# A 480-byte unused tile beside the pre-split weights of the last stage, and that stage's four raw-block pools in the opposite order of SBUF

## The chip, the cores and the metric

The kernel runs on one core of a Trainium2 chip. The metric is the device time of one execution in microseconds (us); the median of three runs is given. The core has five instruction queues that run side by side and wait for each other by semaphores: TensorE (PE, matrix products), VectorE (DVE), ScalarE (ACT), GpSimd (POOL) and SyncE (SP, which here only issues transfers). SP and POOL issue DMA transfers strictly in the order of their queues: an issue that waits holds up every issue behind it. The working memory SBUF has 128 partitions; a place in it is given below as a byte address along the partition. Matrix products accumulate in PSUM.

## The reference

The output is the sum of the input, a spectral mixing of the normalised input, and a gated feed-forward layer of it, all in float32 with 2048 tokens, 640 features and 1728 hidden units:

```
xn = layernorm(x)
a, b = xn @ hid_re.T, xn @ hid_im.T
A = seq_re @ a - seq_im @ b
gate, up = xn @ W_gate, xn @ W_up
B = ((gate * (gate > 0)) * up) @ W_down
out = x + A + B
```

## The kernel before

Every float32 product is made from three matmuls of a shorter float format. An operand is split into a high part (a rounding copy, on ACT, line 125) and a low part (the rest, a subtraction on DVE, line 126); then `mm3` (lines 131 to 133) issues high by high, high by low, and low by high. Each of these matmuls has 128 by 128 stationary weights and 512 moving columns. Most products are further cut into seven block products in place of eight (names such as B11, T1, B21, T2, B22, T3, T4).

There are three stages. In the first, the sequence matrices are streamed and multiplied with the normalised tokens. In the second, `gate_up(n)` runs for 26 steps (13 blocks of hidden units for each half `q` of the tokens, first q = 1 and then q = 0), followed by `gate_up_rest(0, 25)` for the 64 left-over hidden units. In the third, `project(q)` multiplies what the first two stages left in DRAM (`pq`, `hd`, `hr`) with the hidden-DFT matrices and W_down, for q = 1 and then q = 0.

**The third stage.** `project` makes a list of units: the seven products in the order B11, T1, B21, T2, B22, T3, T4, each over 7 units (three of the hidden DFT: feature blocks 0-1, 2-3, 4; three of W_down; one `end`). A unit has a `load` (DMAs on SP), a `prepare` (differences and splits on DVE and ACT) and a `run` (matmuls). `drive(4, 2)` writes out the order for SP and POOL: loads four units ahead of the run, prepares two units ahead. The order on PE, DVE and ACT inside this stage is planned when the program is built; that of the second stage is the program order on these three.

A unit's data: a raw block `rw` of 128 x 1024 floats (4096 bytes a partition) in one of four pools `raws0` to `raws3`, six buffers each; its split form `cb` (pool `ring2`); and weights. For B11, T1, B21 and B22 the weights come as raw `wr` (pool `wraw`) and are split by ACT and DVE into `wt` (pool `wts`). For T2, T3 and T4 both parts come ready from DRAM (`wparts`, `wend`, which the second stage wrote through its tiles `pw`), by one DMA into `wd` (pool `wdir`, six buffers of 4096 bytes), and no engine touches them before PE. `y` holds the output blocks and `re` the raw blocks of the unit `end`.

Unit 0 of B11 for q = 1 is special: it is loaded and split early, in the second stage, by `lead_load` and `lead_split`, into the tile `gw` of that stage. So the first load of the third stage is that of unit 1: at line 1102 the raw block of unit 1, then (needed only later, by T1) that of unit 0, and at line 1155 the weights `wr` of unit 1.

**Places.** SBUF is filled from both ends; a pool takes the next bytes on its side. A place of the third stage lies where tiles of the second did, and its first transfer waits for the last use of whatever lay there. Two names occur twice: `wr` is also the left-over weights of the second stage (pool `wr`, read by PE in `gate_up_rest`), and `gw` exists at an even and an odd place. In the program before, the places are:

| second stage | bytes | third stage | bytes |
|---|---|---|---|
| gw, even steps | 2048 to 19456 | wr (raw weights) | 2048 to 14336 |
| st (left stage) | 19456 to 27648 | cb | 14336 to 47104 |
| r1 | 27648 to 60416 | wt | 47104 to 71680 |
| pw, two tiles | 60416 to 84992 | raws0 | 71680 to 96256 |
| p1, u2, u3 | 84992 to 91136 | raws1 | 96256 to 120832 |
| oa | 91136 to 95232 | raws2 | 120832 to 145408 |
| wr (left-over weights) | 95232 to 100352 | raws3 | 145408 to 169984 |
| ob | 100352 to 108544 | wd | 176096 to 200672 |
| z | 108544 to 128000 | y | 200672 to 221152 |
| st (stage3) | 128000 to 136192 | re | 221152 to 229344 |
| sets_b (T2, T1, T3, T4; 8192 each) | 136192 to 168960 | | |
| gw, odd steps | 170496 to 187904 | | |
| xs_early (B and X sets) | 187904 to 228864 | | |
| edge (480 bytes, unused) | 228864 to 229344 | | |

A pool of the third stage hands out its lowest buffer first and then goes from the highest down: for `raws0` 71680, 92160, 88064, 83968, 79872, 75776. Which pool a product's raw blocks take is `place` in `get`: for q = 1 B11, B12, B21, B22 take pools 0, 1, 2, 3; for q = 0 they take 3, 0, 1, 2.

Lines of the profile that the steps below speak of: 122, 125 and 126 (copies and splits), 131 to 133 (`mm3`), 856 (the last use of `oa`, in `finals`), 946, 947 and 950 (`gate_up_rest`: activation, product, store of `hr`), 1013 and 1017 (stores of `pw` to `wparts` and `wend`), 1037 and 1038 (`lead_load`), 1102 and 1108 (raw blocks), 1139, 1151 and 1155 (weights), 1210 (the two-matmul form of the last, short unit), 1233, 1236 and 1240 (`y`: load, addition, store).

Of the kernel before, what the change touches and what calls it, by code (L numbers as in the profile page):

```python
# [7 lines left out]
F32 = mybir.dt.float32  # L8
# [4 lines left out]
P = 128  # L13
# [11 lines left out]
LEDGE, EDGE = 448, 480  # L25
# [10 lines left out]
B11, B12, B21, B22, T1, T2, T3, T4, X4 = range(9)  # L36
# [22 lines left out]
def fnet_reglu_kernel(  # L59
# [490 lines left out]
    def first_stream(c, name, g):  # L550
# [7 lines left out]
        def load():  # L558
            if n == 0 and c == 0:
                st = start["raw"] = [raw(), raw()]  # L560
                get = lambda c, j: nc.sync.dma_start(st[c][:, j * CH : (j + 1) * CH], dft[c, 0, 0][:, j * CH : (j + 1) * CH])
                ln_load(0, slice(0, 1))
                get(0, 0)
                get(1, 0)
                ln_load(0, slice(1, 2))
                get(0, 1)
                get(1, 1)
                return
            if norm is not None:
                tc.keep_in_program_order(ln_load(norm, slice(0, SG)))  # L570
            if n > 0 or c > 1:
                t["s"] = raw()
                nc.sync.dma_start(t["s"], dft[c, 0, n])
                start[c, n] = t
# [191 lines left out]
    for step in range(2, SET_STEPS):  # L766
        load, (make, more), halve = token_sets(1, step)
        c, i = 1 + (step - 2) // 2, step % 2
# [41 lines left out]
    pool = open_pools.__getitem__  # L810
# [273 lines left out]
    ph0.close()  # L1084


    for n, b, side in (("wraw", 4, "left"), ("ring2", 4, "left"), ("wts", 4, "left"), *((f"raws{i}", 6, "left") for i in range(4)), ("ends", 4, "right"), ("y", 1, "right"), ("wdir", 6, "right")):
        open_pools[n] = ctx.enter_context(tc.tile_pool(name=n, bufs=b, side=side, reuse_waits="tile"))

    units = [("hid", u) for u in HID_UNITS] + [("f", u) for u in F_UNITS] + [("end", (NF // 2,))]  # L1090
    a, b2 = slice(0, REST), slice(REST, 2 * REST)
    raws, held = {}, []

    def get(q, kind, u):
        what, ks = units[u]
        place = (("B11", "B12", "B21", "B22").index(kind) + (3 if q == 0 else 0)) % 4
        o = raws[q, kind, u] = (pool("ends").tile([P, 1, CH], F32, name="re") if what == "end" else
                                pool(f"raws{place}").tile([P, 2, CH], F32, name="rw")[:, : len(ks)])
        col, row = int(kind in ("B12", "B22")), int(kind in ("B21", "B22"))
        cs = slice(col * CH, (col + 1) * CH)  # L1100
        if what == "hid":
            nc.sync.dma_start(o, pqd[2 * q + col][row][:, ks[0] : ks[-1] + 1])  # L1102
        elif what == "end" and row:
            if col:
                nc.gpsimd.memset(o[b2], 0.0)
            nc.sync.dma_start(o[a, 0], hrest[q][:, cs])
        else:
            nc.sync.dma_start(o, hd[q][2 * ks[0] + row : 2 * ks[-1] + row + 1 : 2][:, :, cs].rearrange("f p t -> p f t"))
# [211 lines left out]
```

## Time and profile before

| | |
|---|---|
| median of 3 runs | 1031.7 us (1031.12 to 1032.37) |
| the profiled execution, its own time | 1031.89 us |
| its span in the trace | 1030.1 us |
| PE busy | 1023.6 us, 99% of the span |
| weight loads (PEld) busy | 844.0 us, 82% |
| DVE, ACT, POOL busy | 818.1, 433.9, 124.8 us |
| granted TensorE clock | 1.0 |

The span runs from the first to the last recorded work; what lies around it in the profiled execution is 1031.89 - 1030.1 = 1.79 us. A row of the timeline has the start and the length in us, then engine, line, operation and tiles (written <- read). Matmuls overlap in the pipeline, so a row of 0.39 us does not mean that the next one starts 0.39 us later: the distance between two starts is what a matmul costs in a full stream. SPq rows are transfer issues on SP, not the transfers themselves.

### The profile page before, as it was taken

What the parts mean: (1) busy time and instruction counts of PE and PEld (TensorE: products, weight loads), DVE (VectorE), ACT (ScalarE), POOL (GpSimd) and SP (SyncE); (2) the same over time, 40 slices, a digit from 0 to 9 for tenths busy, and PEclk for the clock granted to TensorE, in tenths of its full rate; (3) what the DMA queues carried; (4) which work ended last, traced back from release to release, by engine and by line L of the source; (5) the groups of instructions that cost most, each with busy time, mean ns of one, the idle gap of its engine ahead of it and who ended that gap; (6) DMA issues with size and microseconds to landing.
All of it is one profiled execution on the core that took longest, in us unless ns stands there. A gap on an engine that the chain in (4) does not pass through costs nothing.

```text
span 1030.1 us, 12551 instructions
## 1 busy us (share of the span) xinstructions
PE 1023.6 (99%) x4520; PEld 844.0 (82%) x4520; DVE 818.1 (79%) x1117; ACT 433.9 (42%) x552; POOL 124.8 (12%) x196
## 2 busy tenths in 40 slices
PE   9999999999999999999999999999999999999998
PEld 7888888888888888888888888888788888888886
DVE  7967987998989585888778988886597895767973
ACT  5554453343433333433336434443454434444432
POOL 3531001012110002411100000011000000000000
PEclk9999999999999999999999999999999999999999
DMA  7897734968969784763464766774699467995724
GB/s 299 293 340 263 265 122 164 337 221 265 359 217 346 297 328 158 251 210 139 153 234 154 255 241 240 253 282 161 237 406 306 134 246 233 305 319 175 241 89 136
DMA packets 90525, 249.12 MB, mean 242 GB/s; under 512 B 11232, under 2 KB 30752, under 8 KB 87776
## 3 DMA queue, kind: packets, MB, share of 16 engines
q1 hardware_dynamic: 72288, 174.66, 49.6%
q0 software_dynamic: 18176, 73.67, 19.4%
q8 instruction: 35, 0.57, 0.2%
q14 instruction: 26, 0.21, 0.1%
HBM read 185.63 MB, written 61.62 MB: 240 GB/s over the span
## 4 chain that ended last, share of the span: by engine, by line
PE 99%; DMA 0%; DVE 0%; ACT 0%; SPq 0%; issue 0%
PE ps L131 31%; PE ps L133 31%; PE ps L132 31%; PE ps L498 3%; PE ps L527 1%; PE ps L1210 1%; PE ps L113 1%; DMA wr<-in_hid 0%; ACT wt L125 0%; DVE y L1236 0%; SPq L1102 0%; DVE warm L109 0%; DVE eps_t L103 0%
## 5 line engine op out<-in xcount | busy, mean ns | idle before, releaser
L125 ACT ACTIVATE cb<-rw 128x1024 fp32r<-128x1024 f32 x83 | 81.8, 987 | 136.2 <-PE ps L133 90.8
L126 DVE TENSOR_TENSOR cb<-rw,cb 128x1024 fp32r<-128x1024 f32 x83 | 93.9, 1132 | 50.9 <-ACT cb L125 50.1
L125 ACT ACTIVATE cb<-raw 128x1024 fp32r<-128x1024 f32 x71 | 75.3, 1060 | 114.8 <-PE ps L133 108.4
L126 DVE TENSOR_TENSOR cb<-raw,cb 128x1024 fp32r<-128x1024 f32 x71 | 86.8, 1223 | 40.0 <-ACT cb L125 39.7
L131 PE MATMUL ps<-cb,wt 128*128 128x512 f32 x270 | 105.2, 389 | 1.1 <-ACT wt L125 1.1
L132 PE MATMUL ps<-cb,wt 128*128 128x512 f32 x270 | 105.0, 389 | 0.0
L133 PE MATMUL ps<-cb,wt 128*128 128x512 f32 x270 | 104.9, 389 | 0.0
L131 PE MATMUL ps<-xs_early,gw 128*128 128x512 f32 x260 | 101.2, 389 | 0.0
L133 PE MATMUL ps<-xs_early,gw 128*128 128x512 f32 x260 | 101.2, 389 | 0.0
L132 PE MATMUL ps<-xs_early,gw 128*128 128x512 f32 x260 | 101.1, 389 | 0.0
L122 ACT ACTIVATE gw<-z 128x1024 fp32r<-128x1024 f32 (+1 forms) x52 | 57.7, 1110 | 79.5 <-DVE z L833 78.5
L131 PE MATMUL ps<-cb,xs_late 128*128 128x512 f32 x232 | 90.2, 389 | 0.0
L132 PE MATMUL ps<-cb,xs_late 128*128 128x512 f32 x232 | 90.2, 389 | 0.0
L133 PE MATMUL ps<-cb,xs_late 128*128 128x512 f32 x232 | 90.2, 389 | 0.0
L131 PE MATMUL ps<-cb,xs_early 128*128 128x512 f32 x226 | 87.9, 389 | 0.0
L132 PE MATMUL ps<-cb,xs_early 128*128 128x512 f32 x226 | 87.9, 389 | 0.0
L133 PE MATMUL ps<-cb,xs_early 128*128 128x512 f32 x226 | 87.9, 389 | 0.0
L122 ACT ACTIVATE u<-ps 128x512 f32<-128x512 f32 x52 | 31.1, 598 | 88.8 <-PE ps L133 88.8
L843 DVE TENSOR_TENSOR gw<-z,gw 128x1024 fp32r<-128x1024 f32 (+1 forms) x52 | 64.8, 1284 | 1.3 <-ACT gw L122 1.2
L131 PEld LDWEIGHTS ps<-cb,wt 128*128 128x128 f32 x270 | 50.7, 188 | 12.0 <-ACT wt L125 1.5
L133 PEld LDWEIGHTS ps<-cb,wt 128*128 128x128 f32 x270 | 50.7, 188 | 10.6
L132 PEld LDWEIGHTS ps<-cb,wt 128*128 128x128 f32 x270 | 50.7, 188 | 10.4
(191 smaller groups left out, 2216.3 us busy)
## 6 DMA issues: line engine op xcount, KB each, us to landing
raw<-in_dft SPq DMA_DIRECT2D x94, 512.0 KB, 6.1
z<-in_wgu SPq DMA_DIRECT2D x26, 640.0 KB, 3.9
wd<-wparts SPq DMA_DIRECT2D x30, 512.0 KB, 6.4
wparts<-pw POOLq DMA_DIRECT2D x12, 1152.0 KB, 4.4
hd<-ob POOLq DMA_DIRECT2D x26, 512.0 KB, 3.5
rw<-hd SPq DMA_DIRECT2D x24, 512.0 KB, 7.2
tk<-in_dft SPq DMA_DIRECT2D x16, 512.0 KB, 6.8
set<-r POOLq DMA_DIRECT2D x16, 512.0 KB, 4.0
```

Of the source, the lines that this page charges most:

```text
L113: nc.tensor.matmul(ps[:, :P], warm, warm, start=True, stop=True)
L122: return nc.scalar.activation(o, i, AF.Copy)
L125: nc.scalar.activation(hi, src, AF.Copy)
L126: return nc.vector.tensor_tensor(lo, src, hi.bitcast(F32), op=OP.subtract)
L131: nc.tensor.matmul(ps, wh, mh, start=first, stop=False, skip_group_check=more)
L132: nc.tensor.matmul(ps, wh, ml, start=False, stop=False, skip_group_check=more)
L133: nc.tensor.matmul(ps, wl, mh, start=False, stop=last, skip_group_check=more)
L498: start["pe"] = pin([nc.tensor.matmul(E[0, key], xn_part(n * SG + j, d)[v == 1], b[:, int(v == 2), j], start=False, stop=n % NH == NH - 1 ...
L527: pin([nc.tensor.matmul(E[c, key], xn_part(j, d)[v == 1], b[c][0][:, int(v == 2), j], start=j == 0 and v == 0, stop=False)])
L843: tt(self.w[:, 1, cs], self.z[:, cs], self.w[:, 0, cs].bitcast(F32), op=OP.subtract)
L1210: nc.tensor.matmul(B[out], w[:, 0, v, oo : oo + P], b[:, 0, 0], start=False, stop=last and v == 1, skip_group_check=more)
```

## The change

```diff
-    for n, b, side in (("wraw", 4, "left"), ("ring2", 4, "left"), ("wts", 4, "left"), *((f"raws{i}", 6, "left") for i in range(4)), ("ends", 4, "right"), ("y", 1, "right"), ("wdir", 6, "right")):
+    for n, b, side in (("wraw", 4, "left"), ("ring2", 4, "left"), ("wts", 4, "left"), *((f"raws{i}", 6, "left") for i in range(4)), ("ends", 4, "right"), ("y", 1, "right"), ("edge3", 1, "right"), ("wdir", 6, "right")):
...
+    pool("edge3").tile([P, EDGE // 4], F32, name="edge")
...
-        place = (("B11", "B12", "B21", "B22").index(kind) + (3 if q == 0 else 0)) % 4
+        place = (("B22", "B21", "B12", "B11").index(kind) + (q == 0)) % 4
```

`EDGE` is 480. The tile `edge` of the new pool `edge3` is never written or read; it takes 480 bytes on the right side between `y` and `wdir`, so that the six places of `wd` lie 480 bytes lower, at 175616 to 200192. `y` and `re` stay.

The raw blocks of B11, B12, B21 and B22 take pools 3, 2, 1, 0 for q = 1 and 0, 3, 2, 1 for q = 0: each old pool number p has become 3 - p. The pools themselves, their sizes and the order of loads, splits and matmuls in the program's text are the same.

## The prediction

> **What bounds the kernel now.** I read the busy shares first, then the chain of waits, then the waits of PE alone.
>
> ```profile
> span 1030.1 us, 12551 instructions
> PE 1023.6 (99%) x4520; PEld 844.0 (82%) x4520; DVE 818.1 (79%) x1117; ACT 433.9 (42%) x552; POOL 124.8 (12%) x196
> PE 99%; DMA 0%; DVE 0%; ACT 0%; SPq 0%; issue 0%
> PE ps L131 <- ACT wt L125: 1.1, 1, 1.1
> ```
>
> PE runs for 1023.6 of 1030.1 us, the chain that ended last is PE for 99%, and PE has one wait worth a name: 1.1 us for weights of the last stage. So only two things can move the time: what one matmul costs in the stream, and that wait. The grouping by line and shape shows that the first is not the same everywhere.
>
> ```profile
> L131 PE MATMUL ps<-cb,wt 128*128 128x512 f32 x270 | 105.2, 389 | 1.1 <-ACT wt L125 1.1
> L131 PE MATMUL ps<-xs_early,gw 128*128 128x512 f32 x260 | 101.2, 389 | 0.0
> L131 PE MATMUL ps<-cb,xs_early 128*128 128x512 f32 x226 | 87.9, 389 | 0.0
> L131 PE MATMUL ps<-cb,wd 128*128 128x512 f32 x140 | 55.0, 395 | 0.0
> ```
>
> All large groups take 389 ns a matmul, only those with weights in `wd` take 395. The timeline of PE shows what that is in the stream: here T2 of q = 1 begins, ends and gives way to B22, and here T3 and T4 do.
>
> ```profile
> 805.29 0.39 PE L131 MATMUL ps<-cb,wd 128*128 128x512 f32 x1
> ...
> 821.86 0.39 PE L133 MATMUL ps<-cb,wd 128*128 128x512 f32 x1
> 822.08 0.39 PE L131 MATMUL ps<-cb,wt 128*128 128x512 f32 x1
> ...
> 845.89 0.39 PE L131 MATMUL ps<-cb,wd 128*128 128x512 f32 x1
> ...
> 878.78 0.39 PE L133 MATMUL ps<-cb,wd 128*128 128x512 f32 x1
> 879.01 0.39 PE L131 MATMUL ps<-cb,wt 128*128 128x512 f32 x1
> ```
>
> T2 has 12 weight pairs, each for 2 outputs and 3 matmuls: 72 in 822.08 - 805.29 = 16.79 us, 0.2332 each. T3 and T4 have 72 and 70 (the short unit has 2 for 3): 142 in 33.12 us, 0.2332 again. B22 between them, weights in `wt`, has 11 x 9 + 6 = 105 in 845.89 - 822.08 = 23.81 us: 0.2268. So a matmul with `wd` costs 6.4 ns more.
>
> **The change, part by part.**
>
> *The unused tile.* It adds no instruction and no wait, and it moves `wd` from 176096 to 175616. A weight block is 512 bytes a partition and starts a multiple of 512 inside its tile, in `wd` as in `wt`. Of the table of places, `wt` (47104 = 92 x 512), both `gw` (2048, 170496) and `xs_early` (187904) lie on multiples of 512; 176096 is 480 past one, and 175616 is 343 x 512. The shift thus makes `wd` what all groups at 389 ns are. It isn't the height in SBUF: `gw` of the odd steps and `xs_early` lie on both sides of it, at 389. Bounds for a matmul with the shifted `wd`: 0.2332 (nothing changes) to 0.2268 (the row of `wt`). I take 0.2268, since in every other respect (type, size, stride, moving tile) `wd` is nearest to `wt`, in the same stage. T2: 16.79 - 72 x 0.2268 = 0.46 us; T3 and T4: 33.12 - 142 x 0.2268 = 0.91 us; twice, for both q: **2.75 us**. PE is the bound throughout, so all of it lies on the path; behind it DVE must keep up:
>
> ```profile
> 805.20:822.10 16.90, 16.90 (x75) 13.56 (x74) 14.72 (x18) 9.03 (x11) 1.66 (x3) 1.00 0.63 191
> 822.10:845.90 23.80, 23.80 (x107) 19.70 (x106) 22.34 (x26) 8.98 (x11) 0.00 (x0) 1.00 0.69 248
> 845.90:879.00 33.10, 33.10 (x143) 26.55 (x142) 22.09 (x25) 15.64 (x18) 2.70 (x5) 1.00 0.75 230
> ```
>
> Columns are the stretch, its length, then PE, PEld, DVE, ACT and POOL. DVE has 14.72 of 16.90 us in T2 and 22.09 of 33.10 in T3 and T4, so 0.46 and 0.91 us less still cover it. B22 with 22.34 of 23.80 is the tightest, but its time isn't shortened.
>
> The Trainium skill speaks against this part: "SBUF — State Buffer", section "Specifications (TRN2)", has lines of 16 bytes and a penalty for crossing into a new one. Both addresses are multiples of 16, so by it a block touches as many lines as before, and the gain of this part would be nothing; "TensorE: Matmul & The Clock Gate", section "Part 2: What happens when you issue a matmul", adds that loading the next weights takes no read bandwidth from the running matmul. The trace disagrees in the 6.4 ns, which neither page explains.
>
> *The pools in opposite order, where the second stage ends.* The raw blocks of B11 for q = 1 move from `raws0` to `raws3`. This is where PE's wait of 1.1 us comes from. SP's queue, its waits there, and PE:
>
> ```profile
> 718.81 12.63 SPq L1102 DMA_DIRECT2D rw<-pq  x2
> 731.49 0.43 SPq L1155 DMA_DIRECT2D wr<-in_hid  x1
> 731.96 0.46 SPq L1102 DMA_DIRECT2D rw<-pq  x1
> ...
> SPq L1102 <- DMA wend<-pw: 23.0, 1, 23.0
> SPq L1102 <- DVE ob L856: 8.4, 1, 8.4
> SPq L1102 <- PE ps L133: 3.5, 1, 3.5
> ...
> 723.88 0.39 PE L133 MATMUL ps<-sets_b,gw 128*128 128x512 f32 x1
> ...
> 730.68 0.39 PE L133 MATMUL ps<-xs_early,wr 128*128 128x512 f32 x1
> ...
> 735.01 0.39 PE L133 MATMUL ps<-gw 128*128 128x512 f32 x1
> 736.47 0.50 PE L131 MATMUL ps<-cb,wt 128*128 128x512 f32 x1 [1.07 <-ACT wt L125]
> 736.80 0.39 PE L132 MATMUL ps<-cb,wt 128*128 128x512 f32 x1
> ...
> 731.10 0.33 SPq L1102
> 731.49 4.06 DMA wr<-in_hid
> 735.57 0.85 ACT wt L125
> ```
>
> The first issue (unit 1, place 71680, inside both `pw`) went out at 718.81. The second (unit 0, place 92160 to 96256, across `oa` and the left-over `wr`) stood at the head of the queue until DVE line 856 had read `oa` and the last matmul on the left-over `wr` was done: 731.10, 0.42 us after that matmul's start. The weights of unit 1, whose own place had long been free, were queued behind it, went out at 731.49, took 4.06 us, then 0.85 us on ACT, and PE began late: 736.47 - 735.01 = 1.46 us, and 0.33 to the next, in place of 0.2268 each. That is **1.33 us** lost.
>
> After the change the two raw blocks lie at 145408 (in T1's part of `sets_b`) and 165888 (T4's). The last matmul on any part of `sets_b` starts at 723.88; with the same 0.42 us the queue is free at 724.3 at the latest. The weights are third, and issues follow each other by 0.47 (731.49, 731.96): out at 725.3, and landed at 729.4 by the 4.06 us. ACT gets to them behind its work of the second stage, if their order stays:
>
> ```profile
> 731.11 0.59 ACT L946 ACTIVATE st<-ps 64x512 f32<-64x512 f32 x1 [1.12 <-PE ps L133]
> 731.60 1.05 ACT L125 ACTIVATE cb<-rw 128x1024 fp32r<-128x1024 f32 x1
> ...
> 732.68 1.22 DVE L126 TENSOR_TENSOR cb<-rw,cb 128x1024 fp32r<-128x1024 f32 x1 [0.26 <-ACT cb L125]
> 736.45 0.96 DVE L126 TENSOR_TENSOR wt<-wr,wt 128x768 fp32r<-128x768 f32 x1 [2.54 <-ACT wt L125]
> ```
>
> ACT: high part of the weights from 732.65 to 733.5. DVE: low part from 733.9 to 734.9. PE wants the first at 735.01 + 0.23 = 735.24 and the second two matmuls later, so the wait is gone with 0.8 us to spare. Late next would be the splits of unit 2, but unit 1 gives PE 18 x 0.2268 = 4.1 us. I take the whole 1.33; the other bound is nothing, if ACT's order or another wait keeps PE at 736.47.
>
> *The pools elsewhere.* Inside the stage each old pool p is 3 - p for both q, so the same products follow each other in the same pool, and nothing changes but names. Against the second stage, B12 comes to `raws2`, where only 133120 (its fourth buffer) is late: `stage3`, from which `hr` is stored.
>
> ```profile
> 732.73 0.53 POOL L950 DMA_DIRECT2D hr<-st  x1 [4.24 <-DVE st L947]
> DMA to landing us min/median/max: 5.6/5.6/5.6
> 748.56 0.43 SPq L1108 DMA_DIRECT2D rw<-hd  x1
> ```
>
> The store lands at about 738.3, and the fourth unit of T1, which would now use that place, is loaded at 748.56, so 10 us cover it; uncovered it would cost SP's queue that difference. B21 and B22 come later still. The first `wd` places leave `xs_early` and lie under the odd `gw` alone, long free when they are loaded.
>
> *Sum.* 2.75 + 1.33 = 4.08 us off the profiled execution's 1031.89 (span 1030.1 and 1.79 around it): span 1026.0, execution 1027.8. That execution is 0.2 above the median, so the median becomes 1031.7 - 4.1 = **1027.6 us**.
>
> **The rivals.**
>
> *A. The shift does nothing; only the wait goes.* The 6.4 ns would come from something else that only `wd` has: no other weights are written by DMA alone. For it: the records of weight loads are no longer for `wd` (187 against 188 ns below). Against it: data that landed long ago can't tell who wrote it, and the pitch is 0.2332 in T2 and in T3 with T4, while the DMA share goes from 0.63 to 0.75 and ACT's share falls; contention would vary. Time: 1031.7 - 1.33 = 1030.4. The Trainium skill's line rule, above, gives this same time.
>
> ```profile
> L131 PEld LDWEIGHTS ps<-cb,wd 128*128 128x128 f32 x140 | 26.2, 187 | 6.6 <-DVE y L1236 0.3
> L133 PEld LDWEIGHTS ps<-cb,wt 128*128 128x128 f32 x270 | 50.7, 188 | 10.6
> ```
>
> *B. The wait stays, only the shift works.* The planner could put ACT's splits of unit 1 in another order, or another place could hold the queue as long. Time: 1031.7 - 2.75 = 1028.9.
>
> *C. The queue is held longer: slower.* One mechanism: the first raw block of `raws3` waits not for `sets_b` but for all of the second stage's tiles on that side, the store of `hr` among them (landing 738.3). With R the time of release, the weights go out at R + 0.95; PE's loss is 1.33 + (R + 0.95 - 731.49). It is nil up to R = 729.2, as before at 730.5, eats the gain of the shift at 733.3, and is measurably slower from 735.4. At R = 738.3 the loss grows by 7.8 and the time is 1031.7 - 2.75 + 7.8 = 1036.7. Against it: the present waits are for the very tiles that overlap (`pw`, `oa`, left-over `wr`), and `raws3` touches no part of `stage3` (136192 at most).
>
> *D. Neither part works*: 1031.7.
>
> **How the numbers follow.** Forecast (both) 0.80, A 0.06, B 0.07, C 0.04, D 0.03. A measurement of this kernel can tell about 0.2%, 2.1 us, from no change. Faster by more: forecast and B, 0.87; within: A and D, 0.09; slower: C, 0.04. Range: the runs before spread 0.6 below and 0.7 above their median. Low: 1027.6 - 0.6, and 0.2 since the execution that gives the terms is that much above the median: 1026.8. High: B's 1028.9 + 0.6 = 1029.5. That leaves A, C and D out, 0.13, and the tails.
>
> **What would show it.** Right: groups with `wd` at 389 ns; T2 in 16.3 us; no wait of PE at `wt` near 735; the `wr` issue at about 725. Wrong: `wd` still at 395 (A); PE's wait beside `wt` still 1 us or more, or the second line-1102 issue near 731 (B) or 738 (C); a new wait of PE later in the last stage, where there is none now, would say that the planner's order changed.

## The result and the profile after

| | before | after |
|---|---|---|
| median of 6 runs each | 1031.55 us (1031.00 to 1032.37) | 1027.51 us (1027.01 to 1030.23) |
| ratio, 95% interval | | 0.9964 [0.9951, 0.9976] |
| profiled execution, its own time | 1031.89 us | 1028.00 us |
| its span | 1030.1 us | 1026.1 us |

The forecast was 1027.6 us, span 1026.0. The change saves 0.36% of the time; the interval leaves no change out. After it, the page, the waits of PE and the groups by line and shape read:

```profile
span 1026.1 us, 12548 instructions
PE 1020.0 (99%) x4520; PEld 843.5 (82%) x4520; DVE 817.6 (80%) x1117; ACT 434.8 (42%) x552; POOL 125.1 (12%) x196
...
PE ps L113 <- DVE warm L109: 1.0, 1, 1.0
PE ps L131 <- ACT ob L122: 0.6, 1, 0.6
...
L131 PE MATMUL ps<-cb,wt 128*128 128x512 f32 x270 | 105.0, 389 | 0.0
L131 PE MATMUL ps<-cb,wd 128*128 128x512 f32 x140 | 54.3, 390 | 0.0
```

The groups with `wd` are at the duration of all others, and PE's wait for `wt` has gone. PE is busy for 3.6 us less in as many matmuls. T2 of q = 1 begins and gives way to B22 in the timeline at

```profile
804.02 0.39 PE L131 MATMUL ps<-cb,wd 128*128 128x512 f32 x1
...
820.34 0.39 PE L131 MATMUL ps<-cb,wt 128*128 128x512 f32 x1
```

which is 16.32 us for 72 matmuls, 0.2267 each, where 16.33 was forecast. The start of the last stage, on SP, ACT and PE:

```profile
724.03 0.39 PE L133 MATMUL ps<-sets_b,gw 128*128 128x512 f32 x1
...
724.45 0.81 SPq L1103 DMA_DIRECT2D rw<-pq  x2
725.36 0.38 SPq L1156 DMA_DIRECT2D wr<-in_hid  x1
...
730.39 0.85 ACT L125 ACTIVATE wt<-wr 128x768 fp32r<-128x768 f32 x1 [0.26 <-DMA wr<-in_hid]
731.25 0.60 ACT L946 ACTIVATE st<-ps 64x512 f32<-64x512 f32 x1
...
735.11 0.39 PE L133 MATMUL ps<-gw 128*128 128x512 f32 x1
735.34 0.39 PE L131 MATMUL ps<-cb,wt 128*128 128x512 f32 x1
```

(Lines below the new tile are one higher than before: 1103 is 1102, 1156 is 1155.) The weights of unit 1 go out at 725.36, the forecast was 725.3, and PE goes from the lead's last matmul to unit 1 in 0.23 us.

Two things in these two traces have nothing to do with the change. PE reaches the second stage at 156.96 us before and at 156.22 after, with the same code up to there, and in all twelve experiments it did so between 156.1 and 156.4: that profiled execution of before lost 0.7 us at its start. And after has one wait that before has not:

```profile
451.39 0.50 PE L131 MATMUL ps<-xs_early,gw 128*128 128x512 f32 x1 [0.57 <-ACT ob L122]
```

There a store of `hd` landed late and held ACT back. The two starts around it are 0.96 us apart and the next 0.34, which is 0.84 us lost. The same wait stands at the same place in two of the experiments (1 and 9), a trace of it in two more (4 and 11), and not in the others, whatever their edit. It nearly offsets the 0.7, by chance, so that the difference of the spans, 4.0 us, is still close to the change's own.

### The profile page after: what moved, and what is told of

It reads as the page before. It is cut to its first block, busy times and chain, and to the rows that moved or that the text cites. A ratio compares the mean times of both kernels' runs of the same rounds, so it can differ in the third digit from the quotient of the medians.

```text
span 1026.1 us, 12548 instructions
## 1 busy us (share of the span) xinstructions
PE 1020.0 (99%) x4520; PEld 843.5 (82%) x4520; DVE 817.6 (80%) x1117; ACT 434.8 (42%) x552; POOL 125.1 (12%) x196
## 4 chain that ended last, share of the span: by engine, by line
PE 97%; DMA 1%; DVE 1%; issue 1%; POOL 0%; ACT 0%; POOLq 0%; ACTq 0%
PE ps L131 31%; PE ps L133 31%; PE ps L132 31%; PE ps L498 3%; PE ps L527 1%; DMA hd<-ob 1%; PE ps L1211 1%; DMA r<-in_x 0%; POOL sets_b L389 0%; POOL sets_b L388 0%; DVE ob L856 0%; DVE bs L205 0%; DVE ob L854 0%; DVE y L1237 0%; ACT cb L309 0%
```

## The experiments

All edits are against the changed kernel, unless a line says otherwise. Experiments 1, 2 and 12 ran several times and have a median; the others ran once, and are read by their traces and not by their times.

**1. The unused tile alone.**

```diff
-        place = (("B22", "B21", "B12", "B11").index(kind) + (q == 0)) % 4
+        place = (("B11", "B12", "B21", "B22").index(kind) + (3 if q == 0 else 0)) % 4
```

> The unused tile alone, raw blocks in the old places. My theory (two separate gains): groups with weights in wd at 389 ns as after the whole change, T2 at a pitch of 0.2268, PE's wait of about 1.1 us beside wt back at the start of the last stage with the second line-1102 issue near 731; 2.75 us under the kernel before, 1028.8. Rival (the place order does all of it): wd at 395 ns, no gain. Rival (the wait hides part of the shift or the other way round, so the parts don't add): anything other than about 1.3 us over the whole change.

Measured: 1028.95 us (1028.60 to 1029.93, 10 runs) against 1031.48 for the kernel before on the same chip (20 runs), ratio 0.9974 [0.9965, 0.9983]: 2.5 us. The groups, the wait and SP's queue:

```profile
L131 PE MATMUL ps<-cb,wd 128*128 128x512 f32 x140 | 54.3, 390 | 0.0
...
PE ps L131 <- ACT wt L125: 1.3, 1, 1.3
...
718.44 12.61 SPq L1103 DMA_DIRECT2D rw<-pq  x2
731.10 0.43 SPq L1156 DMA_DIRECT2D wr<-in_hid  x1
```

The matmuls are fast and the wait is there, as expected of two separate gains.

**2. The opposite order of the pools alone.**

```diff
-... ("edge3", 1, "right"), ("wdir", 6, "right")):
+... ("wdir", 6, "right")):
...
-    pool("edge3").tile([P, EDGE // 4], F32, name="edge")
```

> The opposite order of the four pools alone, wd left at 176096. My theory: wd at 395 ns and T2 at a pitch of 0.2332 as before, no wait of PE at wt, first weights of the last stage issued near 725.4; 1.33 us under the kernel before, 1030.2, which is within what a measurement can tell. Rival (the shift does all of it): the wait of 1.1 us stays and the time is that of before.

Measured: 1029.92 us (1029.75 to 1032.88, 11 runs) against the same 1031.48, ratio 0.9988 [0.9979, 0.9997]: 1.6 us. PE has no wait after its start, and

```profile
L131 PE MATMUL ps<-cb,wd 128*128 128x512 f32 x140 | 55.0, 395 | 0.0
...
723.57 0.81 SPq L1102 DMA_DIRECT2D rw<-pq  x2
724.48 0.38 SPq L1155 DMA_DIRECT2D wr<-in_hid  x1
```

the matmuls with `wd` are as slow as before. T2 takes 16.79 us. The two parts give 2.5 + 1.6 = 4.1 us, the whole change 4.0: they add, as far as times with intervals of 0.9 us and more to each side can tell. The traces tell it more sharply: each part alone has its own gain whole and nothing of the other.

**3. The old places, with the weights ahead in SP's queue.** Against experiment 1:

```diff
-                if name == "B11" and (q, "B11", 0) not in raws:
-                    get(q, "B11", 0)
...
                 if name in ("B11", "B21"):
                     nc.sync.dma_start(r, own[name == "B21"][:, :, : 3 * P])
+                    if name == "B11" and (q, "B11", 0) not in raws:
+                        get(q, "B11", 0)
```

> The unused tile with the old places, but the weights of unit 1 are issued on SP ahead of the raw block of unit 0, which still has to wait for the left-over weights. If PE's wait came from the order of SP's queue alone, the weights now go out right after the first raw block, near 719.5, PE doesn't wait at wt, and the span is that of the whole change, 1026.1, though no raw block has moved. If the places matter in another way (a slower read or write of those blocks), the wait of about 1 us stays and the span is near 1027.4.

Measured: span 1025.4 us, no wait of PE at `wt` (the 0.7 us under the expected 1026.1 is no gain: this trace lacks the 0.84 us that after lost near 451).

```profile
718.35 0.39 SPq L1154 DMA_DIRECT2D wr<-in_hid  x1
730.24 0.80 SPq L1103 DMA_DIRECT2D rw<-pq  x2
731.09 0.42 SPq L1154 DMA_DIRECT2D wr<-in_hid  x1
...
734.15 0.39 PE L133 MATMUL ps<-gw 128*128 128x512 f32 x1
734.37 0.61 PE L131 MATMUL ps<-cb,wt 128*128 128x512 f32 x2
```

The raw block of unit 0 still waits till 730.24 for the left-over weights, and it costs nothing, since the weights of unit 1 went out 12 us earlier. So what before lost at this place was the order in SP's queue alone; the places matter only through what the issue at its head waits for.

**4. B11 of q = 1 in pool 1.**

```diff
-        place = (("B22", "B21", "B12", "B11").index(kind) + (q == 0)) % 4
+        place = (("B11", "B12", "B21", "B22").index(kind) + (q == 1)) % 4
```

> The unused tile, with the raw blocks of B11 for q = 1 in pool 1 and the others one further. The first buffer there, 96256, lies in the left-over weights, so now the first issue waits for the last matmul of the second stage and the weights are third. By the formula of the prediction with release at 731.1: weights out at 732.05, PE loses 1.33 + 0.56 = 1.9 us where it lost 1.33 before, and nothing in the whole change: span near 1028.0. If the wait comes from something other than the release of the place, the loss is 0 or 1.33 and the span near 1026.1 or 1027.4.

Measured: span 1028.5 us, which is 0.5 more than the formula gave; PE's loss is larger than 1.9.

```profile
730.38 0.81 SPq L1103 DMA_DIRECT2D rw<-pq  x2
731.24 0.42 SPq L1156 DMA_DIRECT2D wr<-in_hid  x1
...
731.24 5.33 DMA wr<-in_hid
736.60 0.85 ACT wt L125
...
734.27 0.39 PE L133 MATMUL ps<-gw 128*128 128x512 f32 x1
737.49 0.50 PE L131 MATMUL ps<-cb,wt 128*128 128x512 f32 x1 [2.84 <-ACT wt L125]
737.83 0.40 PE L132 MATMUL ps<-cb,wt 128*128 128x512 f32 x1
```

The loss is 3.22 + 0.34 - 2 x 0.2267 = 3.1 us. The mechanism is the expected one: the first issue now waits for the last matmul of the second stage, and the weights are third. They went out 0.49 us later than before when counted from the lead's last matmul (731.24 - 734.27 against 731.49 - 735.01). The formula had 0.56 for that. What it left out is that the transfer takes 5.33 us and not 4.06, with two raw blocks of 512 KB just ahead of it where before had one: 1.27 us. 1.34 + 0.49 + 1.27 = 3.1. The number of raw blocks ahead shows in all the traces: this transfer takes 4.06, 4.27 and 4.22 us in before and in experiments 1 and 3, with one just ahead of it, and 4.99 to 5.33 us in the eleven others, with two. That the span is only 0.5 over the forecast is because this trace, too, lacks most of the wait near 451.

**5 to 8. Which starts are slow, and for which operand.** In 5 and 6 only the unused tile's size differs; in 7 and 8 other tiles move as well.

```diff
-    pool("edge3").tile([P, EDGE // 4], F32, name="edge")
+    pool("edge3").tile([P, 8], F32, name="edge")
```

> The whole change with an unused tile of 32 bytes in place of 480: wd lies at 176064 = 2751 x 64, a multiple of 64 but not of 128. If what counts is a multiple of 64 (my guess: 512 bytes of weights then touch 8 pieces of 64 bytes and not 9), wd is at 389 ns and T2 of q = 1 takes 16.33 us, span 1026. If it takes 128, 256 or 512, wd stays at 395 ns, T2 at 16.79 us, span 1028.8.

```diff
-    pool("edge3").tile([P, EDGE // 4], F32, name="edge")
+    pool("edge3").tile([P, 112], F32, name="edge")
```

> The whole change with an unused tile of 448 bytes: wd lies at 175648, only 32 bytes above the place of the change, past a multiple of 64 by 32 again. If alignment is the cause, wd is back at 395 ns, T2 at 16.79 us, span 1028.8. If the cause was the place as such (what lies there, or the buffer that no longer reaches into xs_early: its place now ends at 187936, 32 bytes inside), or the distance to y, wd stays at or near 389 ns; a smaller offset than 480 of 512 would show as something between.

```diff
-... ("ring2", 4, "left"), ("wts", 4, "left") ...
+... ("ring2", 4, "left"), ("edge4", 1, "left"), ("wts", 4, "left") ...
...
+    pool("edge4").tile([P, 8], F32, name="edgew")
```

> The whole change, and 32 unused bytes between ring2 and wts, so that wt (and the raw blocks behind it) lie 32 past a multiple of 64. wt is written by ACT and DVE, not by DMA. If the place of the weights is the cause whoever wrote them, wt goes to 395 ns, its 834 matmuls cost 6.4 ns more each, 5.3 us, span 1031.4, and B22 of q = 1 takes 23.81 + 0.67 us. If only weights that a DMA wrote are slow off the grid (rival A), wt stays at 389 and the span at 1026.1.

```diff
-... ("ring2", 4, "left"), ("wts", 4, "left") ...
+... ("edge4", 1, "left"), ("ring2", 4, "left"), ("edge5", 1, "left"), ("wts", 4, "left") ...
...
+    pool("edge4").tile([P, 8], F32, name="edgem")
+    pool("edge5").tile([P, 120], F32, name="edgew")
```

> The whole change, with 32 unused bytes ahead of ring2 and 480 behind it: the moving tiles cb lie 32 past a multiple of 64, wt and wd on the grid. If only the weights' place counts, all groups stay at 389 ns and the span near 1026.1. If the moving operand counts alike (2048 bytes: 33 pieces in place of 32, once a matmul), the 1262 matmuls of the last stage with cb cost up to 6.4 ns more, up to 8 us.

Measured, in the groups by line and shape: the tile of 32 bytes (first fence), the tile of 448 bytes (second), `wt` moved by 32 (third), `cb` moved by 32 (fourth).

```profile
L131 PE MATMUL ps<-cb,wd 128*128 128x512 f32 x140 | 54.6, 393 | 0.0
L132 PE MATMUL ps<-cb,wd 128*128 128x512 f32 x140 | 55.1, 394 | 0.0
L133 PE MATMUL ps<-cb,wd 128*128 128x512 f32 x140 | 54.4, 388 | 0.0
```

```profile
L131 PE MATMUL ps<-cb,wd 128*128 128x512 f32 x140 | 55.0, 395 | 0.0
```

```profile
L131 PE MATMUL ps<-cb,wt 128*128 128x512 f32 x270 | 106.8, 395 | 0.0
L131 PE MATMUL ps<-cb,wd 128*128 128x512 f32 x140 | 54.3, 390 | 0.0
```

```profile
L131 PE MATMUL ps<-cb,wt 128*128 128x512 f32 x270 | 106.7, 395 | 0.0
L131 PE MATMUL ps<-cb,wd 128*128 128x512 f32 x140 | 55.0, 395 | 0.0
```

Weights that ACT and DVE wrote, moved by 32 bytes, are as slow as `wd` was, and B22 of q = 1 takes 24.49 us, 0.68 more than before, where 0.67 was expected (span 1031.0, expected 1031.4): rival A's reason, that only weights written by DMA are slow, has fallen. A shift by 448 in place of 480 bytes, into nearly the same place, gains nothing, so it is the start and not the neighbourhood. The multiple of 64 was a wrong guess: two of the three matmuls of a product are still slower, and T2 takes 16.48 us, a third of the way back to the 16.79 of before. And the moving operand counts too, which I hadn't thought likely: with `cb` 32 bytes off, all groups of the last stage are at 395, and the span is 1033.6, 7.5 us over after's.

**9 to 11. Multiples of 128, and small offsets.** In the last two, the buffers are 4224 bytes and lie on multiples of 128; the weights start 16 or 4 bytes in. The edit of 11 is shown against 10, and in both the line of `wd` that reads `wend` changes in the same way.

```diff
-    pool("edge3").tile([P, EDGE // 4], F32, name="edge")
+    pool("edge3").tile([P, 24], F32, name="edge")
```

> The whole change with an unused tile of 96 bytes: wd lies at 176000 = 1375 x 128, a multiple of 128 but not of 256. The multiple of 64 before gave T2 in 16.48 us, a third of the way from 16.32 to 16.79. If 128 is the grid, T2 takes 16.32 us and all wd groups 389 ns, span 1026. If it takes 256 or 512, T2 stays at or above 16.48.

```diff
-    pool("edge3").tile([P, EDGE // 4], F32, name="edge")
+    pool("edge3").tile([P, 24], F32, name="edge")
...
-... .tile([P, 2 * 4 * P], F32R, name="wd")[:, : n * 4 * P]
+... .tile([P, 2 * 4 * P + 32], F32R, name="wd")[:, 4 : 4 + n * 4 * P]
```

> The whole change, with wd buffers of 4224 bytes on multiples of 128, in which the weights start 16 bytes in. If the loss comes with any start off the grid, T2 takes 16.79 us as with 32 bytes, span 1028.8. If what counts are lines of 16 bytes (the Trainium skill, SBUF — State Buffer, Specifications (TRN2)), 16 bytes cost nothing and T2 takes what it takes on the multiple of 128. If the loss grows with the offset, T2 lies between.

```diff
-... .tile([P, 2 * 4 * P + 32], F32R, name="wd")[:, 4 : 4 + n * 4 * P]
+... .tile([P, 2 * 4 * P + 32], F32R, name="wd")[:, 1 : 1 + n * 4 * P]
```

> As the run before, with the weights 4 bytes in. A grid of any size from 16 bytes up gives a loss: T2 at 16.79 us by a grid of which the start alone counts. If 4 bytes cost nothing, the loss isn't one of crossing pieces.

Measured, with the earlier ones: T2 of q = 1, from its first start to the first of B22, as a mean for each of its 72 matmuls:

| start of the weights past a multiple of 512 | T2, us | per matmul, ns |
|---|---|---|
| 480 (before) | 16.79 | 233.2 |
| 0 (the change) | 16.32 | 226.7 |
| 448 | 16.48 | 228.9 |
| 384 | 16.74 | 232.5 |
| 32 | 16.80 | 233.3 |
| 16 past 128, 256, 384 or 0, by the buffer | 16.32 | 226.7 |
| 4 past these | 16.71 | 232.1 |
| 0, but the moving tile 32 | 16.80 | 233.3 |

None of the grids that I proposed holds. 384 is a multiple of 128 and nearly as slow as 480, while 16 bytes past such multiples is fast, in buffers that differ in their multiple of 128. Nor does the loss grow with the offset. The run with 16 bytes shows why a rule of addresses alone can't do: the same six buffers are fast in T3 of q = 0 and slow in its T4. The groups of that run between 990 and 1006 us (first two rows), and between 1007 and 1022 (last two), and the break between them on the timeline:

```profile
L131 PE MATMUL ps<-cb,wd 128*128 128x512 f32 x24 | 9.3, 389 | 0.0
L132 PE MATMUL ps<-cb,wd 128*128 128x512 f32 x24 | 9.3, 389 | 0.0
...
L132 PE MATMUL ps<-cb,wd 128*128 128x512 f32 x19 | 7.5, 395 | 0.0
L131 PE MATMUL ps<-cb,wd 128*128 128x512 f32 x18 | 7.1, 396 | 0.0
...
1005.84 0.39 PE L133 MATMUL ps<-cb,wd 128*128 128x512 f32 x1
1006.06 0.67 PE L131 MATMUL ps<-cb,wd 128*128 128x512 f32 x2
1006.57 0.40 PE L132 MATMUL ps<-cb,wd 128*128 128x512 f32 x1
```

At 1006.06 two matmuls take 0.51 us to the next start, not 0.453: a stall of 0.06 us, where a weight load waits for DVE's additions to `y`. From there to the end of the kernel the stream goes at 233 ns a matmul. The changed kernel has the same stall at the same place. There six distances between starts are longer (228 to 236 ns), and then it is back at 227, so that its groups read:

```profile
L132 PE MATMUL ps<-cb,wd 128*128 128x512 f32 x19 | 7.4, 389 | 0.0
L131 PE MATMUL ps<-cb,wd 128*128 128x512 f32 x18 | 7.0, 390 | 0.0
```

So the same starts can go with both paces. But the stall doesn't always change the pace: in T4 of q = 1 the run with 16 bytes has the same stall, 0.51 us for two matmuls, and goes on at 0.227, with nothing slow behind it (first two rows). Nor does it take a stall: in the run with 4 bytes, the first eleven distances in T2 of q = 1 sum to 2.50 us, 0.227 each, and the next eleven to 2.56, 0.233 each (last three rows), with no wait of PE or of its weight loads at 805.73.

```profile
860.94 0.67 PE L131 MATMUL ps<-cb,wd 128*128 128x512 f32 x2
861.45 0.39 PE L132 MATMUL ps<-cb,wd 128*128 128x512 f32 x1
...
803.23 0.39 PE L131 MATMUL ps<-cb,wd 128*128 128x512 f32 x1
...
805.73 0.40 PE L133 MATMUL ps<-cb,wd 128*128 128x512 f32 x1
...
808.29 0.39 PE L132 MATMUL ps<-cb,wd 128*128 128x512 f32 x1
```

The matmul behind 805.73 is the first with the weights of T2's second unit, in another buffer. The 232.1 ns of this run in the table are thus a mean of fast and slow stretches. With 448 and 384 they are not: there the distances repeat in a fixed pattern, 229, 232, 226 and 241, 232, 231, 232, 228, 230, 232 ns. What decides between the paces isn't shown. (The run at 384 also has the wait near 451 us of the result's section, 1.8 us lost there by the starts, which is in its span of 1029.6.)

**12. The lead split earlier.** PE has one small wait left at the end of the second stage, for the low parts that `lead_split` makes.

```diff
+            if n and c == 0:
+                lead_split()
             cs = slice(c * CH, (c + 1) * CH)
             nc.scalar.activation(rg[a, cs], ps[b], AF.Relu)
             tt(hh[a, cs], ps[a], rg[a, cs], op=OP.mult)
-            if n and c == 0:
-                lead_split()
```

> The whole change, with lead_split placed ahead of the activation of the first column half in gate_up_rest(0, 25). In the changed kernel PE's starts beside gw at 731.28, 731.58 and 731.92 are 0.19 us longer apart than two matmuls, since the low parts of the lead are ready at 731.5. ACT is free from 725.1 to 727.9 there, so the splits would be done some 2 us earlier: those starts at 0.2268 apart, 0.2 to 0.4 us off the span, 1025.8 by the profiled execution; not told apart by the times. If moving them delays the left-over product instead, PE waits for a PSUM place or the hr store and the span doesn't fall.

Measured: 1026.96 us (1026.81 to 1026.99, 5 runs) against 1031.88 for the kernel before on that chip (9 runs), ratio 0.9949 [0.9935, 0.9962]. ACT:

```profile
724.24 1.78 ACT L125 ACTIVATE gw<-st 128x1024 fp32r<-128x1024 f32 x2
727.09 0.60 ACT L948 ACTIVATE st<-ps 64x512 f32<-64x512 f32 x1 [1.07 <-PE ps L133]
```

The lead's splits run in ACT's idle time, over 3 us earlier (after: 728.35, in a trace that runs 0.76 us later at this place), all starts of PE beside `gw` are 0.2267 apart, which gives 0.2 us, and the span is 1025.2. Most of the 0.9 us under after's span is again the wait near 451, which this trace hasn't. It has the lowest median, but its interval overlaps that of the change (0.9951 to 0.9976), so it isn't shown to be faster than the change.

## Why the prediction was right

*The unused tile.* Right in place and size: 2.75 us forecast; alone it measured 2.5 by the medians, with an interval from 1.8 to 3.6 (ratio 0.9965 to 0.9983 of 1031.5). By the traces of before and after, T2 got 0.47 us shorter for the 0.46 forecast, and T3 with T4 0.85 for 0.91, with the stall of 0.06 us in it: 2.64 for both q. The argument, by the nearest rows (`wt`, `gw`, `xs_early`, all on multiples of 512), picked the right bound. It left open which grid counts, and the experiments didn't find one: they show that the start of a tile sets the pace and that these multiples of 512 are fast, not that 512 is the rule. Nor did it speak of the moving operand, whose start counts as much (experiment 8); the change didn't move it.

*The wait.* Right in mechanism, place and size: 1.33 us forecast, 1.34 by the starts in the trace of before and none after; 1.6 measured alone, with an interval from 0.3 to 2.2 (ratio 0.9979 to 0.9997 of 1031.5). Experiment 3 shows the cause with no raw block moved, and experiment 4 brings the wait back in another place.

*Two steps that were wrong without cost.* The prediction let the weights land at 729.4, by the 4.06 us of before. They went out as forecast, but took 5.02 us and landed at 730.37, with two raw blocks now just ahead of them and not one. And it assumed that ACT keeps its order and takes the weights after line 946 and the raw block's split, from 732.65; the planner put the split of the weights ahead of line 946, at 730.39. The high part was done at 731.24 and PE wanted it at 735.34, so neither mattered here.

*The formula of rival C* has the same 4.06 us in it: it counts the delay of the release and not that the transfer gets longer with what is ahead of it. Where experiment 4 tried it, it gave 1.9 us for 3.1.

*The rivals.* A (the shift does nothing) and B (the wait stays) are refuted by the trace of after itself and by experiments 1 and 2. C is refuted by the first issue at 724.45: it comes 0.42 us after the start of the last matmul on `sets_b` (724.03), the lag that the prediction took from before.

*The rule of 16-byte lines* (the Trainium skill, "SBUF — State Buffer", section "Specifications (TRN2)") would have made offsets of 32, 384, 448 and 480 as good as 0, and the runs show losses of 5.8 to 6.6 ns a matmul at three of them and 2.2 at 448. With 16 and 4 bytes T2 agrees with it: 16 costs nothing, 4 costs 5.4 ns. T4 of q = 0 doesn't: at 16 bytes it is slow.

## What to carry to other kernels

Where PE is busy for 99%, compare its groups by the names of both operands: 6 ns in 389 were worth 2.6 us, more than the only wait of PE in that stage, and they came from where a tile starts. Give stationary and moving tiles a start that the fast groups of the same trace have, and look at the distances through a whole stretch, behind a stall above all, not only at its first ones.

Where two stages share SBUF, read each new tile's place against the last reader of what lies there, in the order of the issuing queue. When the order changes, count a transfer's time with what is now queued ahead of it: one more raw block of 512 KB made it about 1 us longer here. A transfer that isn't urgent, but waits at the head, delays every one behind it; swapping two issues or two places both cured that here.

## What the runs showed of the hardware that was not expected

The start of a tile sets the pace of the matmul stream, here at a granted clock of 0.999 to 1.0 in every run: 226.7 ns from start to start for 128 x 512 where both operands are on multiples of 512, and up to 233.3 at other starts. Either operand can cause the slower one, at the same price: weights 32 bytes off, or the moving tile 32 bytes off (T2 16.80 us in both). Starts don't settle it alone: with weights 16 bytes past multiples of 128, one stall of 0.06 us was followed by the slow pace to the end, 15 us later, and another was not. On multiples of 512 slow matmuls also follow a stall, but they pass: before, the five distances from 736.80 to 737.96, behind the wait near 735, are 228 to 236 ns, and then they are 226 or 227 again. What in the weight loads and reads makes the slow pace isn't known from these runs: the recorded weight loads are 187 to 188 ns in all of them. Whether the distance between the two operands' starts counts, rather than each start, was not tried.
